# Six DMA issues on SyncE made to wait for an earlier transfer's landing, in a fused linear-attention and gated-FFN kernel

## The chip, the core and the metric

The kernel runs on one core of a Trainium2 chip. The metric is the device time of one execution in microseconds (us). The core has five engines that run side by side: TensorE (PE, matmuls, with its weight loads listed as PEld), VectorE (DVE), ScalarE (ACT), GpSimd (POOL) and SyncE (SP), which here issues all DMA transfers of data.

## The reference

A linear attention with a decaying state is followed by an FFN with a convolution gate:

```python
# r, k, v: (4, 8, 768, 48); w, u: (8, 48)
for t in range(S):
    cur = einsum('bhd,bhe->bhde', u * k[t], v[t])
    y[t] = einsum('bhd,bhde->bhe', r[t], state + cur)
    state = w * state + einsum('bhd,bhe->bhde', k[t], v[t])
x = y.transpose(0, 2, 1, 3).reshape(4, 768, 384)
h = maximum(x @ w_in, 0)                  # w_in: (384, 1024)
c = sum(conv_w[j] * shift(h, j - 1) for j in range(3))   # along the sequence
out = (h * sigmoid(c)) @ w_out            # w_out: (1024, 384)
```

All is float32; the weights reach the chip as 64-bit words.

## The kernel before

**Tiling.** The sequences are cut into 24 groups of 128 positions (four batches of six), each of two chunks of 64. For a group the kernel loads the decayed products' inputs: KR (keys and queries with the head dimension on the partitions, 448 KB), and KV (keys and values with positions on the partitions; a value half is 96 KB, a pair of key and query halves 192 KB). Three buffers of each rotate. `prep` scales KR on DVE and makes keys and diagonal terms, `scores`, `additions` and `outputs` give the 64-column matmuls on PE (L494), `chain` carries the state, and `split` copies the result as a high and a low part into XT (L548 on ACT, L549 on DVE).

**The FFN** runs over 7 units of up to 510 positions and 8 slices of the hidden dimension: `first` (L580) multiplies XT with w_in, ACT and DVE make relu, convolution and gate, and `second` (L609) multiplies with w_out, three slices later. The weights come in 8 pieces of w_in (two DMA halves of 192 KB) and 8 of w_out (384 KB) into the three buffers ST. `convert` turns each piece into float32 on ACT (L348, L354, L364), DVE (L356, L358) and DVE or POOL (L207). All pieces are loaded and converted in the first 70 us, between the attention of the first groups.

**What sets the order.** Every operation is recorded by `Plan.op` with a number. The table ORDER, written out by hand, lists these numbers; a letter behind a number picks the engine where several can do it. `Plan.order` reads the table, and a loop at the end of `rwkv_ffn_kernel` emits the operations one by one. Each engine runs its own in the order in which they come. Every data DMA goes through L211 on SP, in the table's order, so an issue that has to wait holds all later ones. An issue waits for the engines that still use its buffer. It also waits for the eighth last issue to have landed, since the issues take turns on eight semaphores (DMAHW0 to DMAHW7).

**Names.** In the rows below `KR<-in_krd_dram`, `KV<-in_vt_dram`, `KV<-in_krt_dram`, `ST<-in_w_in_dram`, `ST<-in_w_out_dram` and `uu<-in_ut_dram` are these loads. `HP<-DW,KR` (L393), `psY<-KR,SS` and `PO<-RS,KV` (L494) are attention matmuls of the first groups, `HP<-XT,wi` (L580) is the FFN's first product.

Of the kernel before, what the change touches and what calls it, by code (L numbers as in the profile page):

```python
# [61 lines left out]
144 277a 117 276 130p 119 128 293a 334 143 292 151d 297 191 335 129a 278 126 274d 279 294 125 213 149 192 341 193 148
295 194 296p 131 195 214 215 152 138p 134 216 132 196 280p 133a 197 135 217 169p 259 139 165 168 147 170p 218 140a 219
260 137 281 261 154p 141 299a 171 220 262 298 157p 155 263 337a 360 300 264 164 282 265 336 221d 198 366 338 283 199d
343a 325 166 158 161 284 159p 359 342 162 172p 163 266 160 305 156 403 326 176p 304 167 285 301 267p 303 327 339 348
328 286 340p 329 173a 174 287 344 302d 347 183 186d 330 350 361 249 189p 331 178 181 175 362a 182 187p 177 368a 349
421 179 288 394 180 185 367 351 404 289d 352 369 235 395 363 345 353 396 346p 364 397 370 373 251 254p 354 240 372 252
355 241 374 365p 332 188 409 244 405a 356 410 190p 237 246 238a 242 423a 357 422 243 247 333d 245 411 358p 412 413 429
427 428 406 371d 459 460 458 239 257p 398 399 236 400 414 407 415 416 417 401 449 255p 308p 256 258a 408p 418 461 424
419 425 402p 470 471 250 315 184 248 316 253 306 472 317 384 385 314 318 450 451 462 463 426p 420p 516 320p 452 453  # L70
454 464 465 466 455 456 467 468 517 501 502 513 519 510 321p 469p 309 310d 323d 307 311 503 312 377a 319 313 514 520
521 375 504 505 322 387 383 440 386 439 389p 457p 530 522 523 511 528 557 506 378 507 548 381 524 382 525 560 379d 388
324a 508 549 550 392p 380 376 430 438 441 551 552 553 390p 444p 391 554 590 509p 559 432d 393d 443 433 561 436 526 562
555 434a 431 437 435 563 591 592 593 564 565 483 445p 447p 571 529 558 473 479 475a 491 442 492 515 556p 496p 497d
499d 566 567 480 594 446 527p 595 476 477p 495 596 478 570 600 602 601 569 599 611 613 448a 481 474 482 531 543p 603
604 597 598p 568d 644 656 642 605 606 498 607 608 609 500p 533p 532 535 536 494 490 542 534 486 485 484 493 488 487
489 539 518 581 512 537 538 540 541 633 634 635 636 637 610p 546p 544p 667 545 645 646 572 624 582 579 612 583 638 639
685 654 700 643 655 694 697 647 648 649 650 574 651 703 547p 686 687 577 695 573 584 585p 586d 588p 640 652 641p 580
653p 628p 629p 575d 576 688 689 690 578 587 691 616a 614 734 701 698 713 714 712 617 704 705 706 707 692 693d 631d 708
709 746 744 627 756 735 736 620 618a 737 619 738 621 589p 630 615 747 748 743 699 676 623 622 675 626 625 702 739 710  # L80
729d 749 740 657 724 777 745 678 725 677 674 663 680p 681p 659p 750 664 670 671 668 751 752 682 732p 632p 683p 711p
757 789 787 741 778 665 666 660 779 780 781 661p 662 679 742p 799 658 755 786 782 790 791 717a 730p 792 793 783 794
715 721 718 753 795 722 728 719a 772p 773p 684p 673 672 669 818 830 775d 720 716 731 760p 754p 758 819 796 820 784 774
821 822 823 824 785p 831 832 761 833 834 797p 733d 759 762p 763 764 835 836 788 828 840 825 868 869 870 767 723 771
776a 800 829 841 798 883 886 887 826d 803d 726 768 765 770 769 809 766 727 801 858 827 839 808 813p 871 872 812 814d
816p 873 888 874 889 917 837 805 815 890 817p 838p 891 875 918 919 880 810 807 696 863p 866p 864p 806 802 804 842 847
849 907 859 908 955p 958p 912p 920 921 892 865 848 862 877 884 844 881 878 922 913p 956p 860 855 854 811 852 856 851
857 879 853 929 923 930 897 895 928 896 960 927 876d 940 931 932 933 924 934 935 972 926 938 893 894d 961 845a 962 850
# [12 lines left out]
1208 1226 1227 1228 1229 1197p 1238 1239 1240 1230 1231 1211 1222 1223 1232 1235 1236 1234 1185 1156 1155 1158 1188
1154 1241 1209p 1242 1243 1233d 1153 1182 1157 1249 1250 1251 1252 1253 1254 1261 1247 1259 1248 1255 1262 1244 1263
1264 1273 1271 1260 1246 1265 1266 1256 1257p 1267 1294 1274 1275 1276 1277 1245p 1278 1268 1295 1296 1279 1297 1298
1272 1286 1287 1289 1306 1299 1269p 1307 1308 1309 1310 1300 1311 1258 1280 1270 1282 1283 1290 1291 1318 1293 1292
1288 1281p 1312 1330 1304 1305 1316 1303 1315 1327 1319 1320 1321 1322 1331 1323 1301 1324 1313 1325 1332 1342 1343
1344 1333 1326d 1334 1345 1346 1328 1302p 1339 1314p 1317 1351 1354 1329 1340 1341 1352 1335 1336 1347 1337 1338p 1355
1358 1348 1349 1350d 1363 1353 1357 1364 1360 1284 1285 1361 1356 1359 1365 1366 1362 1367 1368
"""


class Plan:
# [29 lines left out]
    def order(self):  # L141
        seq, where, done = [], [None] * len(self.ops), set()
        for word in ORDER.split():
            if word == "f":
                seq.append(-1)
                continue
            i = int(word.rstrip("adp"))
            dur, x, pred, fn, cls = self.ops[i]
            assert done.issuperset(pred), (i, cls)
            where[i] = {"a": "act", "d": "dve", "p": "pool"}.get(word[-1]) or next(iter(dur))  # L150
            seq.append(i)
            done.add(i)
        assert len(done) == len(self.ops)
        self.seq, self.where = seq, where
        return seq, where


def rwkv_ffn_kernel(tc, krd, krt, vt, wd, ut, w_in, conv_w, w_out, out):
# [4 lines left out]
    with ExitStack() as ctx:  # L163
# [578 lines left out]
```

## Time and profile before

| | |
|---|---|
| median of 3 runs | 295.09 us (294.67 to 295.52) |
| the profiled execution | 298.1 us, its span 296.4 us |
| mean granted TensorE clock | 0.988 of full speed |
| busy: PE, PEld, DVE, ACT, POOL | 282.3, 244.5, 232.7, 192.1, 133.3 us |
| DMA | 37.47 MB, mean 126 GB/s |

The span runs from the first to the last instruction of the program; the execution's own time has some 1.7 us around it. The views used below are these. The page's first part gives each engine's busy time with the number of its instructions, and its third part the DMA queues. A timeline lists an engine's instructions by start, and in brackets how long the engine had been idle and what ended that; "issue" means that no wait in the profile explains the idle time. A view of stretches gives, for each stretch, every engine's busy time with the count of its instructions, then the granted TensorE clock, the DMA engines' busy share and GB/s. A DMA view of a short window lists what packets it holds by queue (q1 carries data, q8 instructions), and the issues in it with the time from issue to landing.

### The profile page before, as it was taken

The numbers are of one execution on the slowest core, as the hardware profiler recorded it, in microseconds if no ns is written. First come the engines' busy times: TensorE is split into PE (matmuls) and PEld (weight loads), VectorE is DVE, ScalarE is ACT, GpSimd is POOL, SyncE is SP. The second block draws the span as 40 slices with busy tenths as digits, with TensorE's granted clock in tenths as the row PEclk, the third lists the DMA queues.
The fourth block names the chain that finished last, engine by engine and source line by source line (L and its number), as shares of the span: only waits on it lengthen the run. The fifth ranks groups of instructions, "written<-read, shape, count | busy, mean of one in ns | idle before, by whom it ended". The sixth has DMA issues, their size and how long they took to land. (4 is left out here: it accounts for less than half of the span.)

```text
span 296.4 us, 10390 instructions
## 1 busy us (share of the span) xinstructions
PE 282.3 (95%) x4368; PEld 244.5 (82%) x4368; DVE 232.7 (79%) x399; ACT 192.1 (65%) x456; POOL 133.3 (45%) x157
## 2 busy tenths in 40 slices
PE   8778899979999999999999999999999999999995
PEld 6678898979998987878787878887888888888894
DVE  5878799997899988798989887896855875665550
ACT  3447499988797744774665666855456656575662
POOL 4111155668776474648762447173132460321321
PEclk9979799999999999999999999999999999999999
DMA  6958997986346667274453556413433000120021
GB/s 177 240 176 214 222 232 182 238 185 176 107 104 186 170 168 193 72 205 103 100 153 105 135 147 171 130 45 106 139 74 97 2 0 17 35 86 0 35 74 55
DMA packets 18642, 37.47 MB, mean 126 GB/s; under 512 B 3874, under 2 KB 10532, under 8 KB 18596
## 3 DMA queue, kind: packets, MB, share of 16 engines
q1 hardware_dynamic: 18596, 36.82, 47.7%
q8 instruction: 34, 0.56, 0.8%
q14 instruction: 12, 0.10, 0.1%
HBM read 30.01 MB, written 4.72 MB: 117 GB/s over the span
## 5 line engine op out<-in xcount | busy, mean ns | idle before, releaser
L580 PE MATMUL HP<-XT,wi 128*128 128x512 f32 (+3 forms) x504 | 111.4, 367 | 3.2 <-DVE SG L592 1.6
L580 PEld LDWEIGHTS HP<-XT,wi 128*128 128x128 f32 x504 | 88.0, 188 | 18.8 <-DVE SG L592 2.7
L609 PE MATMUL PO<-GH,wo 128*128 128x510 f32 (+3 forms) x336 | 102.0, 363 | 0.0
L588 DVE SCALAR_TENSOR_TENSOR CV<-HP,cw,CV 128x510 f32<-128x510 f32 (+3 forms) x112 | 74.9, 672 | 22.7 <-ACT CV L585 21.0
L207 POOL TENSOR_TENSOR GL<-SG,GH 128x510 fp32r<-128x510 f32 (+3 forms) x39 | 45.6, 1177 | 76.9 <-ACT GH L594 60.0
L609 PEld LDWEIGHTS PO<-GH,wo 128*128 128x128 f32 x336 | 61.3, 188 | 8.5
L609 PE MATMUL PO<-GL,wo 128*128 128x510 f32 (+3 forms) x168 | 60.6, 360 | 0.0
L591 ACT ACTIVATE SG<-CV 128x510 f32<-128x510 f32 (+3 forms) x56 | 32.0, 572 | 41.4 <-DVE CV L588 37.1
L592 DVE TENSOR_TENSOR SG<-HP,SG 128x510 f32<-128x510 f32 (+3 forms) x56 | 34.2, 611 | 13.2 <-ACT SG L591 12.7
L494 PE MATMUL psY<-RS,KV 64*48 64x64 f32 x720 | 43.7, 222 | 0.1
L494 PE MATMUL psY<-KR,SS 48*48 48x64 f32 x660 | 40.4, 217 | 0.4 <-issue 0.4
L584 ACT ACTIVATE HP<-HP 128x512 f32<-128x512 f32 (+3 forms) x56 | 29.3, 523 | 16.9 <-PE HP L580 16.3
L585 ACT ACTIVATE CV<-HP,cw 128x510 f32<-128x510 f32 (+3 forms) x56 | 35.1, 626 | 1.3
L594 ACT CAST GH<-SG 128x510 fp32r<-128x510 f32 (+3 forms) x56 | 30.6, 552 | 7.2 <-DVE SG L592 7.2
L609 PEld LDWEIGHTS PO<-GL,wo 128*128 128x128 f32 x168 | 31.6, 188 | 3.8 <-POOL GL L207 0.2
L207 DVE TENSOR_TENSOR KR<-KR,TKR 112x1024 f32<-112x1024 f32 x24 | 33.4, 1391 | 0.4 <-ACT TKR L322 0.4
L494 PEld LDWEIGHTS psY<-RS,KV 64*48 64x48 f32 x720 | 32.7, 122 | 0.5 <-issue 0.5
L494 PEld LDWEIGHTS psY<-KR,SS 48*48 48x48 f32 x660 | 31.0, 121 | 0.5 <-issue 0.5
L494 PEld LDWEIGHTS psA<-KR 48*64 48x64 f32 x704 | 22.3, 135 | 7.5 <-DVE RS L511 2.7
L433 POOL TENSOR_SCALAR_AFFINE_SELECT RS<-QQ 64x512 f32<-64x512 f32 x24 | 16.4, 685 | 23.4 <-DVE QQ L414 13.0
L494 PE MATMUL psA<-KR 48*64 48x64 f32 x704 | 25.5, 221 | 0.9 <-DVE RS L511 0.6
L548 ACT CAST XT<-psY 112x512 fp32r<-112x512 f32 (+9 forms) x27 | 13.8, 515 | 11.7 <-PE psY L494 11.5
(113 smaller groups left out, 358.7 us busy)
## 6 DMA issues: line engine op xcount, KB each, us to landing
KR<-in_krd_dram SPq DMA_DIRECT2D x24, 448.0 KB, 5.0
KV<-in_krt_dram SPq DMA_DIRECT2D x40, 192.0 KB, 4.0
KV<-in_vt_dram SPq DMA_DIRECT2D x48, 96.0 KB, 4.5
ST<-in_w_in_dram SPq DMA_DIRECT2D x16, 192.0 KB, 5.1
ST<-in_w_out_dram SPq DMA_DIRECT2D x8, 384.0 KB, 6.8
XT<-XT SPq DMA_DIRECT2D x24, 64.0 KB, 3.4
out_dram<-OS SPq DMA_DIRECT2D x6, 255.0 KB, 3.3
out_dram<-OS SPq DMA_DIRECT2D x3, 251.0 KB, 2.2
```

The source lines that it names most:

```text
L207: op(eng, d, rd, wr, lambda e: e.tensor_tensor(**kw), cls, port=True)
L433: G.affine_select(out=RS[j][o:o + 64], in_=QQ[j][o:o + 64].unsqueeze(2).broadcast_to([64, NP * 2, C]), pattern=[[0, NP * 2], [1, C]], comp ...
L494: PE.matmul(y, a, b_, start=s0, stop=s1)
L548: op("act", 0.06 + n / 1200.0, [key], cols("X", a + d, b + d), lambda e, xh=xh, v=v: A.copy(xh, v), "XH")
L580: PE.matmul(hp, wi[a][:, j, fs], XT[:, x, j, t], start=(j == 0 and k == 0), stop=(j == 2 and k == 2))
L584: op("act", 0.093 + n / 1200.0, [], [H_], lambda e: A.activation(hp, hp, AF.Relu, scale=1.0 / WS))
L585: op("act", 0.158 + n / 1200.0, [H_, "cw"], [("T", ti)], lambda e: A.activation(t1, hp[:, 1:n + 1], AF.Copy, scale=cw[:, 3 * f + 1:3 * f + ...
L588: op("dve", 0.117 + n * 1.085e-3, [H_, "cw"], [("T", ti)], lambda e, k=k: V.scalar_tensor_tensor(out=t1, in0=hp[:, k:n + k], scalar=cw[:, ...
L591: op("act", 0.11 + n / 1200.0, [("T", ti), "sgt"], [("SG", ti)], lambda e: A.activation(sg, t1, AF.Sigmoid))
L592: op("dve", dps(n), [H_], [("SG", ti)], lambda e: V.tensor_tensor(out=sg, in0=hp[:, 1:n + 1], in1=sg, op=ALU.mult), "GG")
L594: op("act", act(n), [("SG", ti)], [("GH", gi)], lambda e: A.copy(gh, sg))
L609: PE.matmul(PO[m][:, :n], wo[a][:, f, ms], g2[x], start=(f == 0 and k == 0), stop=(f == NF - 1 and k == 2))
```

## The change

A number in ORDER may now carry `w` and a count. Such an operation, a DMA on SP, gets a dependency on an earlier DMA of SP: with `w3` on the third last one before it. It is issued only when that one has landed. Six numbers get one: operations 2, 41, 275 and 121 `w3`, 223 `w5`, 99 `w2`. Sequence, engines and all other numbers of the table are as they were.

```diff
-17 0 26 12 8 15 10 9 1 16 21 4 14 11 20 5 27 23 18 2 22 13 43 19 35 33 3 31 37 44 32 50 34 80 55 79 38 28 39 40 63 29
-58d 41 36 6 71 56 30 74d 59 45 52d 46a 57a 47 201 200 48 75 82a 7 49d 60 51 81 62d 223 83 72 65 207 76 61a 78p 53 222
+17 0 26 12 8 15 10 9 1 16 21 4 14 11 20 5 27 23 18 2w3 22 13 43 19 35 33 3 31 37 44 32 50 34 80 55 79 38 28 39
+40 63 29 58d 41w3 36 6 71 56 30 74d 59 45 52d 46a 57a 47 201 200 48 75 82a 7 49d 60 51 81 62d 223w5 83 72 65 207
...
-        self.ops, self.port, self.last_w, self.last_r = [], [], {}, {}
+        self.ops, self.port, self.last_w, self.last_r, self.back = [], [], {}, {}, {}
...
+            word, _, back = word.partition("w")
             i = int(word.rstrip("adp"))
+            if back:
+                self.back[i] = int(back)
...
+        sent = []
         with tc.manual_schedule(engines={x.engine for x in eng.values()}):
...
-                    plan.ops[i][3](eng[where[i]])
+                    ins = plan.ops[i][3](eng[where[i]])
+                    if where[i] == "sp":
+                        sent.append(ins.ins)
+                        if i in plan.back:
+                            tc.add_manual_dep(ins.ins, sent[-1 - plan.back[i]].name, mybir.DependencyInfo(
+                                mybir.DependencyClass.Sync, mybir.DependencyReason.DATA), reason="pace")
```

On PE, DVE, ACT and POOL the same instructions stand in the same order with the same waits. On SP the order is the same too, and only the waits differ. Of SP, from the second KR load on (KR1 for the second group, KV0 to KV2 the buffers of the first three), before:

```order
L211 DMA KR1_62<-in_krd_dram 112x1024
L211 DMA KV0_64<-in_vt_dram 64x384
L211 DMA ST0_95<-in_w_in_dram 64x768
...
L211 DMA ST2_97<-in_w_in_dram 64x768 [waits DMAHW1_49]
L211 DMA ST2_97<-in_w_in_dram 64x768 [waits DMAHW2_49]
L211 DMA KR2_63<-in_krd_dram 112x1024 [waits DMAHW3_49]
L211 DMA KV2_66<-in_vt_dram 64x384 [waits DMAHW4_49]
L211 DMA KV1_65<-in_vt_dram 64x384 [waits DMAHW5_49]
```

and now:

```order
L217 DMA KR1_62<-in_krd_dram 112x1024
L217 DMA KV0_64<-in_vt_dram 64x384 [waits DMAHW1_49]
L217 DMA ST0_95<-in_w_in_dram 64x768
...
L217 DMA ST2_97<-in_w_in_dram 64x768
L217 DMA ST2_97<-in_w_in_dram 64x768 [waits DMAHW2_49]
L217 DMA KR2_63<-in_krd_dram 112x1024 [waits DMAHW3_49]
L217 DMA KV2_66<-in_vt_dram 64x384 [waits DMAHW4_49,DMAHW1_49]
L217 DMA KV1_65<-in_vt_dram 64x384 [waits DMAHW5_49]
```

The KV0 load waits for the first KR load (DMAHW1), which the first w_in half of ST2 then needn't name again; the KV2 load waits for that w_in half, the next user of DMAHW1.

Of SP some 20 issues later, at the w_out load of ST2 and the uu behind it, before:

```order
L211 DMA KV1_65<-in_krt_dram 64x768 [waits DMAHW1_49,PE_49]
L211 DMA KV1_65<-in_krt_dram 64x768 [waits PE_49]
L211 DMA ST2_97<-in_w_out_dram 128x768 [waits DMAHW3_49,Activation_49]
L211 DMA uu_123<-in_ut_dram 64x192 [waits DMAHW4_49]
...
L211 DMA KR1_62<-in_krd_dram 112x1024 [waits DMAHW0_49,PE_49]
L211 DMA KV0_64<-in_vt_dram 64x384 [waits DMAHW1_49]
```

and now:

```order
L217 DMA KV1_65<-in_krt_dram 64x768 [waits DMAHW1_49,PE_49]
L217 DMA KV1_65<-in_krt_dram 64x768 [waits PE_49]
L217 DMA ST2_97<-in_w_out_dram 128x768 [waits DMAHW3_49,DMAHW0_49,Activation_49]
L217 DMA uu_123<-in_ut_dram 64x192 [waits DMAHW4_49,DMAHW1_49]
...
L217 DMA KR1_62<-in_krd_dram 112x1024 [waits PE_49]
L217 DMA KV0_64<-in_vt_dram 64x384 [waits DMAHW7_49]
```

The w_out load waits for the w_in half three issues before it (DMAHW0), the uu load for the first of the two KV loads, and the KV0 load for the issue two before it (DMAHW7).

## Rows read from the trace of the kernel before

**Rows 1.** The page, parts 1 (busy us) and 3 (packets, MB, share).

```profile
PE 282.3 (95%) x4368; PEld 244.5 (82%) x4368; DVE 232.7 (79%) x399; ACT 192.1 (65%) x456; POOL 133.3 (45%) x157
...
q8 instruction: 34, 0.56, 0.8%
```

**Rows 2.** Timeline of PE: start us, us, instruction, idle before it.

```profile
15.95 0.37 PE L393 MATMUL HP<-DW,KR 48*64 48x48 f32 x5 [2.98 <-issue]
...
21.47 0.26 PE L494 MATMUL psY<-KR,SS 48*48 48x64 f32 x2 [0.39 <-issue]
...
30.43 0.21 PE L494 MATMUL PO<-RS,KV 64*48 64x64 f32 x1 [1.83 <-issue]
...
66.61 0.62 PE L580 MATMUL HP<-XT,wi 128*128 128x384 f32 x2 [1.49 <-POOL wi L207]
```

**Rows 3.** Stretches from the start: PE busy (x), PEld busy (x), then DVE, ACT, POOL.

```profile
0.00:8.49 8.49, 7.20 (x95) 5.60 (x97) 4.73 (x14) 3.00 (x7) 3.39 (x17) 1.00 0.73 186
...
0.00:12.95 12.95, 11.51 (x222) 9.56 (x222) 8.53 (x22) 5.63 (x15) 3.39 (x17) 1.00 0.82 201
...
0.00:29.00 29.00, 23.79 (x603) 21.44 (x604) 21.32 (x46) 14.26 (x42) 7.54 (x25) 0.94 0.77 200
0.00:186.43 186.43, 175.83 (x3266) 154.58 (x3269) 162.15 (x281) 128.28 (x326) 100.54 (x125) 0.98 0.65 165
```

**Rows 4.** DMA queues, window 13.2 to 13.4; none of q8 from 8.4 to 13.2.

```profile
q8 instruction: 1, 0.02, 39.4%
```

**Rows 5.** DMA queues, window 27.5 to 27.7; none of q8 from 25.0 to 27.5.

```profile
q8 instruction: 1, 0.02, 36.8%
```

**Rows 6.** DMA queues, window 187.1 to 187.3; none of q8 from 171.6 to 187.1.

```profile
DMA packets 1, 0.02 MB, mean 82 GB/s; under 512 B 0, under 2 KB 0, under 8 KB 0
...
q8 instruction: 1, 0.02, 38.8%
```

**Rows 7.** Stretches after the three stops: after five engines, granted clock, DMA share, GB/s.

```profile
16.00:22.00 6.00, 5.61 (x151) 5.46 (x154) 5.03 (x9) 3.07 (x9) 0.91 (x2) 0.72 0.57 178
30.00:36.00 6.00, 5.57 (x145) 5.57 (x146) 3.95 (x8) 1.88 (x7) 1.27 (x1) 0.72 0.93 217
65.00:70.00 5.00, 3.51 (x20) 3.39 (x20) 3.17 (x7) 3.36 (x8) 4.78 (x6) 1.00 0.42 96
```

**Rows 8.** Timeline of SP: issues by start, with the issue's own time.

```profile
1.28 0.40 SPq L211 DMA_DIRECT2D KR<-in_krd_dram  x1
...
2.81 0.53 SPq L211 DMA_DIRECT2D KV<-in_vt_dram  x1
...
5.93 1.10 SPq L211 DMA_DIRECT2D ST<-in_w_in_dram  x2
7.49 0.32 SPq L211 DMA_DIRECT2D KR<-in_krd_dram  x1
7.88 1.28 SPq L211 DMA_DIRECT2D KV<-in_vt_dram  x2
```

**Rows 9.** Tile KR, 0 to 10 us: the three loads, from issue to landing.

```profile
DMA to landing us min/median/max: 3.4/5.0/5.9
```

**Rows 10.** DMA issue of 5.93: KB, us to landing.

```profile
ST<-in_w_in_dram SPq DMA_DIRECT2D x1, 192.0 KB, 4.9
```

**Rows 11.** DMA issue of 19.33, on an empty queue: KB, us to landing.

```profile
ST<-in_w_out_dram SPq DMA_DIRECT2D x1, 384.0 KB, 3.1
```

**Rows 12.** Stretches, columns as in rows 3 and 7.

```profile
15.17:36.10 20.93, 17.93 (x530) 17.55 (x530) 15.44 (x30) 10.92 (x34) 3.73 (x7) 0.84 0.77 201
...
18.00:24.00 6.00, 5.61 (x166) 5.46 (x166) 4.70 (x12) 2.68 (x10) 0.85 (x2) 0.78 0.42 107
24.00:46.00 22.00, 19.47 (x440) 18.32 (x435) 19.13 (x36) 17.37 (x52) 8.40 (x11) 0.92 0.98 237
...
36.00:66.00 30.00, 28.25 (x577) 25.97 (x572) 29.33 (x56) 29.05 (x79) 16.78 (x18) 1.00 0.93 215
```

**Rows 13.** Timeline of DVE, the XT subtraction of the third group.

```profile
36.10 0.56 DVE L549 TENSOR_TENSOR XT<-psY,XT 128x384 fp32r<-128x384 f32 x1 [2.12 <-ACT XT L548]
```

More of the change, by code (lines that the diff above doesn't have):

```diff
@@ L62 @@
[L62 to L76, printed above, removed]
@@ new lines @@
+112 111 121w3 230 212p 231d 113a 24 25 227 97 291 270 114 290 232 115a 271d 122 233 136 272 116a 120 234d 99w2
+228d 118 145 150d 273 153d 146 127 100 142 144 277a 117 276 130p 119 128 293a 334 143 292 151d 297 191 335 129a
+278 126 274d 279 294 125 213 149 192 341 193 148 295 194 296p 131 195 214 215 152 138p 134 216 132 196 280p 133a
+197 135 217 169p 259 139 165 168 147 170p 218 140a 219 260 137 281 261 154p 141 299a 171 220 262 298 157p 155
+263 337a 360 300 264 164 282 265 336 221d 198 366 338 283 199d 343a 325 166 158 161 284 159p 359 342 162 172p
@@ new lines @@
+163 266 160 305 156 403 326 176p 304 167 285 301 267p 303 327 339 348 328 286 340p 329 173a 174 287 344 302d 347
+183 186d 330 350 361 249 189p 331 178 181 175 362a 182 187p 177 368a 349 421 179 288 394 180 185 367 351 404
+289d 352 369 235 395 363 345 353 396 346p 364 397 370 373 251 254p 354 240 372 252 355 241 374 365p 332 188 409
+244 405a 356 410 190p 237 246 238a 242 423a 357 422 243 247 333d 245 411 358p 412 413 429 427 428 406 371d 459
+460 458 239 257p 398 399 236 400 414 407 415 416 417 401 449 255p 308p 256 258a 408p 418 461 424 419 425 402p
@@ new lines @@
+712 617 704 705 706 707 692 693d 631d 708 709 746 744 627 756 735 736 620 618a 737 619 738 621 589p 630 615 747
+748 743 699 676 623 622 675 626 625 702 739 710 729d 749 740 657 724 777 745 678 725 677 674 663 680p 681p 659p
+750 664 670 671 668 751 752 682 732p 632p 683p 711p 757 789 787 741 778 665 666 660 779 780 781 661p 662 679
+742p 799 658 755 786 782 790 791 717a 730p 792 793 783 794 715 721 718 753 795 722 728 719a 772p 773p 684p 673
+672 669 818 830 775d 720 716 731 760p 754p 758 819 796 820 784 774 821 822 823 824 785p 831 832 761 833 834 797p
@@ new lines @@
+915d 1037 925p 1152 965 966 969 939 898 882 906 950 1003 936 973 974 867a 975 861 951 976 977 911 937d 967 968p
+900a 901 978 904 1004 1005 899 957 914 902d 981 970 1015 1016 979 1012 971 983 905 1006 1007 903 1008 941 993
+949 952 980p 998p 954 1009 943d 1050 910 909 1010 944 1017 1018 959p 916p 947 1019 1011d 1020 1021 1051 1052
+1053 1054 942 945p 982 1014 1026 1071 1024 1059 1055 1060 1013 1025 1063 1072 1073 946 997 948 984 986p 1074
+1075 1056 987 988d 1022 1023p 1064 990 985 1076 1077 991 989 1061 1067 1080 1083 1078 1084 1085 1081 1001d 953
@@ new lines @@
+1027 1033 994 1045d 885 1068 1086 1087 1034 1088 1035 1057 1089 1058p 1101 1082 1092 1094 1113 1093 1102 1103
+1104 1105 1106 1079p 1107 1108 1114 1115 1116 992 1125 1112 1111 1124 1110 1122 1090 1091p 1029a 1117 1036 1118
+1119 1126 1127 1040 1070 1038 1042 1066 1041 996 1039 1069 1062 1043 1044 999d 1030 1031p 1032 1137 1138 1136
+1123 1128 1129 1120 1130 1131 1135 1134 1097p 1109p 1046p 1147 1148 1139 1132 1140 1141 1000 1133d 1142 1143
+1144 1145p 1048p 1159 1160 1161 1171 1172 1121d 1146 1168 1180 1169 1002d 1028 1162 1163 1164 1173 1165 1189
@@ new lines @@
+1174 1175 1047 995 1095 1183 1166 1176 1167p 1049p 1177 1201 1096 1099 1100 1065 1190 1191 1181 1192 1098 1193
+1194 1170 1186 1149 1187 1195 1213 1198 1184 1210 1199 1202 1203 1204 1205 1206 1196 1214 1150 1207 1151 1225
+1200 1212 1215 1216 1217 1178 1179p 1224 1218 1219 1237 1220 1221d 1208 1226 1227 1228 1229 1197p 1238 1239 1240
+1230 1231 1211 1222 1223 1232 1235 1236 1234 1185 1156 1155 1158 1188 1154 1241 1209p 1242 1243 1233d 1153 1182
+1157 1249 1250 1251 1252 1253 1254 1261 1247 1259 1248 1255 1262 1244 1263 1264 1273 1271 1260 1246 1265 1266
@@ new lines @@
+1256 1257p 1267 1294 1274 1275 1276 1277 1245p 1278 1268 1295 1296 1279 1297 1298 1272 1286 1287 1289 1306 1299
+1269p 1307 1308 1309 1310 1300 1311 1258 1280 1270 1282 1283 1290 1291 1318 1293 1292 1288 1281p 1312 1330 1304
+1305 1316 1303 1315 1327 1319 1320 1321 1322 1331 1323 1301 1324 1313 1325 1332 1342 1343 1344 1333 1326d 1334
+1345 1346 1328 1302p 1339 1314p 1317 1351 1354 1329 1340 1341 1352 1335 1336 1347 1337 1338p 1355 1358 1348 1349
+1350d 1363 1353 1357 1364 1360 1284 1285 1361 1356 1359 1365 1366 1362 1367 1368
```

51 lines of the change are left out of this document (17 added, 34 removed).

## The prediction

> **What bounds the kernel now.** I read the page first: TensorE (PE) is busy for 95% of a span of 296.4 us, so what is lost on it is lost at the end [rows 1]. The same page lists a DMA queue of its own for instructions, q8: 34 packets, 0.56 MB. PE executes 4368 matmuls and 4368 weight loads, 8736 in all: 257 for each packet. So q8 brings PE its own program, in blocks of about 256.
>
> Then I looked for the places at which PE stands still. Its timeline shows three stops that end in "issue", that is, with no wait that the profile knows: 2.98 us before 15.95, 0.39 before 21.47, 1.83 before 30.43 [rows 2]. Counting PE's instructions explains them: 444 had run at the first stop (222 and 222) and 1207 at the third, 763 more, which is three blocks of 256 less the semaphore waits that the view leaves out [rows 3]. PE stops at block ends, because the next block has not come.
>
> When is a block asked for? Where no data is on the way, the packet follows the start of the block before it at once: 6535 instructions (444 and 24 blocks, less their waits) had run at 186.43, and the window from 187.1 holds a packet and nothing else [rows 3, 6], some 0.7 us later. At the first stop 192 had run by 8.49, one block less than at 12.95 [rows 3]; yet the packet starts only in the window from 13.2 [rows 4], 4.7 us later. What lay ahead is on SP's timeline: 448 KB of KR issued at 7.49 and two KV transfers from 7.88 [rows 8]. The third stop has the same pattern: its packet starts in the window from 27.5 [rows 5]. So program blocks queue behind data that was issued too early.
>
> The stops cost twice. In 16 to 22 us and in 30 to 36 us the granted clock was 0.72 of full speed, between its two levels of 1.2 and 2.4 GHz: 6 us times 0.28 is 1.7 us each time. After the idle of 1.49 us that ended at 66.61 it stayed at 1.00 [rows 2, 7]. In all 2.98 + 0.39 + 1.83 + 1.7 + 1.7 = 8.6 us of PE.
>
> **The change part by part.** No instruction moves and none is added on an engine; six DMA issues on SP get one wait more, and some older waits fall away as implied. SP issues in order, so all that stands behind a held transfer is held too.
>
> *First wait* (the first KV half waits for the first KR). That KR is issued at 1.28 and lands 3.4 us later, at 4.7 [rows 8, 9], so the KV goes out at 4.7 and not at 2.81. Behind it on SP stand four issues of about 0.6 us and the pair at 5.93; the train ends near 8.9 and not at 7.03, 1.9 us later. The KR of 7.49 leaves at about 8.9. Cover: the second KR, issued before it, has 448 KB and keeps the queue busy for 1.9 us after the first one's landing, at 237 GB/s [rows 12], to 6.6; a transfer moves about 1.5 us after its issue (3.1 us to land on an empty queue, less 1.6 us for its 384 KB [rows 11, 12]), the held KV at 6.2. So the data lands as before.
>
> *Second wait* (KV of 7.88 waits for the first w_in half of 5.93). That one lands 4.9 us after its issue, at 10.8 [rows 10]; both KV transfers leave from 10.8 and not from 7.88. In front of them KR2 is then still moving, so again nothing runs dry. Behind them stand the two w_in halves of the next piece, up to 1.9 us later than before. ScalarE, which reads them, was busy for 10.92 of the 20.93 us from 15.17 to 36.10 [rows 12] and can make this up; I take nothing, with 1.9 us as the bound.
>
> What both do together: at 8.49, when PE asks for its block, neither KR2 nor the two KV transfers are on the queue. They are 448 + 192 = 640 KB, at 237 GB/s [rows 12] 2.7 us. The packet should start near 10.6 instead of 13.3. *Term 1:* the stop of 2.98 shrinks by 2.7 to 0.3 us. *Term 2:* an idle of 1.49 us left the clock at 1.00 and one of 2.98 did not, so with 0.3 the slow stretch of 16 to 22 us goes as well: 1.7 us. Together 4.4 us.
>
> *Third wait* (a w_in half, op 223, waits for that KV). The KV itself and four more issues of 0.6 us stand before it, so SP gets there near 13.8. The KV lands at 13.9 if it takes the 3.1 us of an empty queue [rows 11], at 15.7 if it takes 4.9 us as in [rows 10]: a hold of 0.1 to 1.9 us, for a weight piece with the same half idle reader. I take zero.
>
> *Fourth and fifth* (a w_out, op 275, and the uu behind it, op 121), *sixth* (a KV half, op 99). The fourth leaves 384 KB in flight, 1.6 us of work; the sixth 448 KB, 1.9 us. A transfer on an empty queue lands after 3.1 us, 1.5 of which nothing moves, so the worst holes, if nothing else is queued, are 3.1 - 1.6 and 3.1 - 1.9, 2.7 us in all; the best is zero. DMA was busy for 0.98 of 24 to 46 [rows 12], so a backlog covers most of it: I take 0.5. The fifth hides behind the fourth, whose 384 KB are then in flight too. Whether these waits help the third stop the trace can't say, since what lies ahead of that packet moves with everything else. Bounds: 0 and 1.83 + 1.7 = 3.5 us; I take 0, the nearest row being the stop as it is [rows 2, 5].
>
> **What limits the gain.** VectorE (DVE) was busy 15.44 of the 20.93 us from 15.17 to 36.10, so it can follow by 5.5 us at most. DMA was busy 0.42 of 18 to 24, idle for 3.5 us, and then nearly full to 46. From 36 to 66 ScalarE (29.05 of 30) and DVE (29.33) are full too [rows 12]: they run the weights' conversion, fed by DMA. They keep a head start, but only as far as DMA delivers: 3.5 us is all that can be pulled into the idle. So the sum is 4.4, capped at 3.5, less 0.5 for holes: **3.0 us**. From 66 on PE sets the pace and passes this on to the end.
>
> The profiled execution took 298.1 us, 1.7 more than its span, and the runs shown have a median of 295.09. 298.1 - 3.0 = 295.1 for the profiled one; from the median, **292.1**. Should the 3.0 us between the two lie in the stops, 5.6 of the 8.6 us are there without a profile, and the gain is 2.0: 293.1.
>
> **A rule against it.** The packet of 13.3 came after the data issued before it [rows 4, 8]. The Trainium skill, DMA: Bandwidth & Descriptors, section "Queues, rings and completion order", says that each DMA engine takes turns between its queues packet by packet; by that a block would not wait behind another queue's data. The Trainium skill, Runtime: NRT & Kernel Launch, section "Instruction fetch mechanics", gives blocks of 16 KiB, which the trace bears out (0.56 MB in 34), and calls their cost mostly hidden, which the 2.98 us contradict. By these rules the sum would be 0.
>
> **The rivals.**
> - *The packets take turns and do not queue behind data.* The stop then has another cause, and earlier or later issues change nothing: gain 0, cost 0 to 0.5, 295.1 to 295.6. Against it: 0.7 us on a quiet queue and 4.7 on a full one. Chance 0.05.
> - *The gain is given back.* PE waits again before 66.61 for a weight piece from GpSimd [rows 2]; if that is tied to DMA, full by then, the head start only lengthens this wait. Time 294.4 to 295.9. Chance 0.18.
> - *Slower: holes in a full queue.* If pulled-forward use thins the backlog, the fourth and sixth wait each leave DMA dry for 1.2 to 1.5 us in a stretch whose transfers feed full engines: 2.7 us lost. It decides once the gain left by the other stops is below 1.8 us, for instance when the block after the first meets the held KV transfers and PE stops there instead. Then 295.1 - 0.5 + 2.7 = 297.3. Chance 0.13.
> - *More:* the third stop goes too, and the gain reaches DVE's 5.5 us: 289.6. Chance 0.12.
>
> **How the numbers follow.** Forecast 292.1, its own band 290.3 to 294.2, chance 0.52. About 0.3% (0.9 us) is what a measurement of this kernel can tell from no change. Faster: 0.52 + 0.12 = 0.64; within: 0.05 + 0.18 = 0.23; slower 0.13. The range takes in the larger gain and the case given back: 289.5 to 295.9.
>
> **What would show it.** In the changed kernel's trace the first q8 packet should start near 10.6, the stop of 2.98 be under 0.6 and the clock in 16 to 22 us be 1.00; the XT subtraction on DVE at 36.10 [rows 13] should come at 32 to 33. If the packet stays near 13, term 1 is wrong; if it moves and the clock still falls, term 2. If DMA is clearly below 0.98 between 24 and 46 the holes are real; if the PE wait before 66.61 grows by the gain, the second rival holds.

## The result, and the profile after

The changed kernel takes **298.65 us** (median of 9 runs, 296.76 to 300.26); the kernel before took 295.26 beside it (9 runs, 293.90 to 296.39). The ratio is **1.011, 95% interval 1.0074 to 1.0147**: 3.2 us slower, where 3.0 us faster was predicted. The sign was wrong, and the time lies above the range (289.5 to 295.9). Here and below a ratio compares only executions within 1.5% of the fastest of their kernel, which leaves out more of before's than of the others', so it can lie up to 0.3% above the quotient of the medians (e14: 1.0089, medians 296.90 and 295.14).

The profiled execution of the changed kernel took 298.26 us (span 296.6), that of before 298.1 (span 296.4). The two pages can therefore hardly differ, and yet the kernels do: the profile of before shows an execution 3 us above its median, the profile after one at its own. A trace of the changed code without any of the six waits (e1, below: 294.2 us, span 292.5) is the better partner, and stands beside it here. One thing in it is not alike: its first 37 matmuls took 3.11 us and those of after 4.09 (last section), so about 1 us of what separates the two traces does not come from the waits. A second trace of the changed kernel (e9: 2.88 us there, span 295.8) is given where that matters.

The page of after, parts 1 and 3, which answers to [rows 1]:

```profile
PE 283.0 (95%) x4368; PEld 244.6 (82%) x4368; DVE 234.0 (79%) x399; ACT 192.4 (65%) x456; POOL 132.9 (45%) x157
...
q8 instruction: 34, 0.56, 0.8%
```

The DMA queues of after in the window 9.4 to 9.6; no q8 packet lies between 0 and 9.3. It answers to [rows 4], where the packet came at 13.2 to 13.4:

```profile
q8 instruction: 1, 0.02, 35.6%
```

The timeline of PE in after: every idle time of 0.3 us and more between 8 and 47 us (start, duration, instruction, idle before it), which answers to [rows 2]:

```profile
15.65 0.33 PE L500 MATMUL psY<-RS,VP 64*64 64x64 f32 x4 [0.60 <-DVE RS L517]
18.94 0.87 PE L500 MATMUL HP<-KV 64*48 64x48 f32 x29 [1.01 <-DMA KV<-in_vt_dram]
23.05 1.97 PE L500 MATMUL PO<-KR 48*64 48x64 f32 x32 [0.66 <-ACT QQ L415]
33.47 1.13 PE L399 MATMUL psU<-DW,KR 48*64 48x48 f32 x32 [1.11 <-DVE SS L536]
45.12 1.84 PE L586 MATMUL HP<-XT,wi 128*128 128x384 f32 x9 [2.03 <-DVE SG L598]
```

No line says "issue" any more: the program arrives in time, as meant. In place of the three stops of before (2.98 + 0.39 + 1.83 = 5.20 us) stand five waits for data and for the engines that work on it: 0.60 + 1.01 + 0.66 + 1.11 + 2.03 = 5.41 us. (Before has one such wait too, 0.65 us at 45.11, shown further down.) The last one has a cause that can be read off. PE waits for SG; DVE makes SG (L598) right after its product KR (L213), and that one waited for a load. DVE in after, then SP in after (when it issued what):

```profile
43.04 1.56 DVE L213 TENSOR_TENSOR KR<-KR,TKR 112x1024 f32<-112x1024 f32 x1 [1.06 <-DMA KR<-in_krd_dram]
```

```profile
24.20 1.18 SPq L217 DMA_DIRECT2D KV<-in_krt_dram  x2
28.77 0.33 SPq L217 DMA_DIRECT2D ST<-in_w_out_dram  x1
...
32.73 0.58 SPq L217 DMA_DIRECT2D KR<-in_krd_dram  x1
35.05 0.47 SPq L217 DMA_DIRECT2D KV<-in_vt_dram  x1
...
38.05 0.53 SPq L217 DMA_DIRECT2D KR<-in_krd_dram  x1
```

Two holes stand in SP's line: 25.38 to 28.77, the fourth wait (op 275, w_out), and 33.31 to 35.05, the sixth (op 99, KV). The KR load of the sixth group is issued at 38.05. In e1, without these holes, it goes out at 32.00, and DVE does not wait. SP, then DVE, of e1:

```profile
32.00 0.33 SPq L217 DMA_DIRECT2D KR<-in_krd_dram  x1
```

```profile
40.43 1.39 DVE L213 TENSOR_TENSOR KR<-KR,TKR 112x1024 f32<-112x1024 f32 x1
```

e9, the changed kernel again, with the shorter first matmuls, has the same chain. DVE, then PE, of e9:

```profile
42.67 1.57 DVE L213 TENSOR_TENSOR KR<-KR,TKR 112x1024 f32<-112x1024 f32 x1 [0.94 <-DMA KR<-in_krd_dram]
```

```profile
44.76 1.84 PE L586 MATMUL HP<-XT,wi 128*128 128x384 f32 x9 [1.72 <-DVE SG L598]
```

Stretches of after (after the five engines: granted clock, DMA share, GB/s), then of e1:

```profile
12.00:16.00 4.00, 3.40 (x122) 3.29 (x120) 2.94 (x6) 2.13 (x9) 1.68 (x2) 1.00 0.49 144
...
20.00:28.00 8.00, 7.34 (x169) 7.18 (x167) 7.40 (x16) 5.39 (x17) 2.07 (x5) 0.57 0.88 223
28.00:30.00 2.00, 2.00 (x76) 2.00 (x74) 0.97 (x3) 1.21 (x4) 0.00 (x0) 1.00 0.31 70
...
36.00:38.00 2.00, 2.00 (x16) 1.75 (x15) 1.75 (x4) 1.97 (x5) 0.00 (x0) 1.00 0.59 157
24.00:46.00 22.00, 18.57 (x404) 17.55 (x401) 18.67 (x35) 16.86 (x51) 9.61 (x13) 0.92 0.81 207
```

```profile
12.00:16.00 4.00, 3.35 (x114) 3.12 (x112) 3.41 (x7) 2.59 (x10) 2.12 (x3) 1.00 1.02 237
...
28.00:30.00 2.00, 1.72 (x60) 1.57 (x56) 1.97 (x5) 1.67 (x6) 0.00 (x0) 1.00 0.92 239
30.00:36.00 6.00, 4.68 (x44) 4.59 (x45) 5.00 (x9) 3.18 (x8) 1.27 (x1) 0.72 1.03 238
36.00:38.00 2.00, 2.00 (x34) 1.75 (x34) 1.36 (x3) 1.86 (x5) 0.66 (x1) 1.00 1.01 203
```

The holes are there as DMA share: 0.49, 0.31 and 0.59 in after, where e1 has 1.02, 0.92 and 1.01. From 24 to 46 it is 0.81, against 0.98 in [rows 12] and 0.95 in e1; but e15, a second trace without any wait, has 0.83 there, so this mean alone shows no holes, and SP's timeline has to. And the clock still falls, to 0.57 from 20 to 28, which costs 8 × 0.43 = 3.4 us, as much as the two slow stretches of [rows 7] (1.7 each).

All of the difference from e1 is made in the first 79 us. PE of e1, then of after, the same feed-forward matmuls:

```profile
42.34 1.85 PE L586 MATMUL HP<-XT,wi 128*128 128x384 f32 x9 [0.53 <-DVE SG L598]
...
74.75 1.86 PE L586 MATMUL HP<-XT,wi 128*128 128x388 f32 x9 [0.34 <-DVE SG L598]
```

```profile
78.80 1.51 PE L586 MATMUL HP<-XT,wi 128*128 128x388 f32 x7 [0.55 <-DVE SG L598]
```

After is 2.8 us behind e1 at 45.12 (about 1 us of it from the first matmuls), 4.05 at 78.80, and 4.1 at the end (296.6 less 292.5). e9 is 2.4 us behind at its 44.76.

Beside the traced execution of before, the same matmul shows where the head start goes. DVE of after at the subtraction of [rows 13], then PE of before:

```profile
33.79 0.55 DVE L555 TENSOR_TENSOR XT<-psY,XT 128x384 fp32r<-128x384 f32 x1
```

```profile
45.11 1.84 PE L580 MATMUL HP<-XT,wi 128*128 128x384 f32 x9 [0.65 <-DVE SG L592]
```

At the subtraction after is 2.31 us ahead (33.79 against 36.10); at the feed-forward matmul, 45.12 against 45.11, all of that is gone.

### The profile page after: what moved, and what is told of

The parts are those of the page before. It is cut to its first block, busy times and chain, and to the rows that moved or that the text cites. A ratio compares the mean times of both kernels' runs of the same rounds, so it can differ in the third digit from the quotient of the medians.

```text
span 296.6 us, 10390 instructions
## 1 busy us (share of the span) xinstructions
PE 283.0 (95%) x4368; PEld 244.6 (82%) x4368; DVE 234.0 (79%) x399; ACT 192.4 (65%) x456; POOL 132.9 (45%) x157
## 5 line engine op out<-in xcount | busy, mean ns | idle before, releaser
L213 POOL TENSOR_TENSOR GL<-SG,GH 128x510 fp32r<-128x510 f32 (+3 forms) x39 | 45.8, 1181 | 77.4 <-ACT GH L600 60.6
L598 DVE TENSOR_TENSOR SG<-HP,SG 128x510 f32<-128x510 f32 (+3 forms) x56 | 34.2, 611 | 13.1 <-ACT SG L597 12.6
L500 PE MATMUL psY<-RS,KV 64*48 64x64 f32 x720 | 42.5, 218 | 0.1
L500 PE MATMUL psY<-KR,SS 48*48 48x64 f32 x660 | 39.6, 215 | 0.0
L213 DVE TENSOR_TENSOR KR<-KR,TKR 112x1024 f32<-112x1024 f32 x24 | 33.5, 1396 | 1.7 <-DMA KR<-in_krd_dram 1.3
L500 PEld LDWEIGHTS psY<-RS,KV 64*48 64x48 f32 x720 | 31.7, 119 | 0.6 <-issue 0.6
L500 PEld LDWEIGHTS psY<-KR,SS 48*48 48x48 f32 x660 | 30.2, 119 | 0.0
L439 POOL TENSOR_SCALAR_AFFINE_SELECT RS<-QQ 64x512 f32<-64x512 f32 x24 | 17.9, 744 | 24.2 <-DVE QQ L420 13.0
L213 POOL TENSOR_TENSOR KV<-KV 128x384 f32<-128x384 f32 x16 | 17.6, 1099 | 7.6 <-DMA KV<-in_krt_dram 4.6
```

The source lines that it names most:

```text
L213: op(eng, d, rd, wr, lambda e: e.tensor_tensor(**kw), cls, port=True)
L439: G.affine_select(out=RS[j][o:o + 64], in_=QQ[j][o:o + 64].unsqueeze(2).broadcast_to([64, NP * 2, C]), pattern=[[0, NP * 2], [1, C]], comp ...
L500: PE.matmul(y, a, b_, start=s0, stop=s1)
L598: op("dve", dps(n), [H_], [("SG", ti)], lambda e: V.tensor_tensor(out=sg, in0=hp[:, 1:n + 1], in1=sg, op=ALU.mult), "GG")
```

## The experiments

All kernels are the changed kernel's code with other waits or another order in its table; everything is computed. "w3" behind an op means that it is issued when the third last transfer before it has landed. Of the table only the words around an edit are shown. Each ratio is to runs of the kernel before on the same chip, with its 95% interval. e16 and e18 have 4 executions, e9 and e10 have 6, the others 10 to 12. The 18 runs:

| run | waits and order | median us | ratio |
|---|---|---|---|
| e1, e15 | none | 294.20, 294.96 | 0.9985 (0.9951 to 1.0018), 1.0029 (0.9988 to 1.0069) |
| e2 | first | 296.19 | 1.0040 (1.0006 to 1.0074) |
| e3 | second | 295.86 | 1.0029 (0.9992 to 1.0067) |
| e4, e18 | fourth to sixth | 297.83, 297.89 | 1.0104 (1.0066 to 1.0142), 1.0110 (1.0034 to 1.0187) |
| e5 | sixth | 296.87 | 1.0055 (1.0026 to 1.0085) |
| e6 | fourth and fifth | 295.82 | 1.0030 (0.9992 to 1.0068) |
| e7, e17 | one, at KR | 296.90, 296.83 | 1.0052 (1.0020 to 1.0084), 1.0081 (1.0042 to 1.0119) |
| e8 | one, behind KR | 295.37 | 0.9999 (0.9965 to 1.0034) |
| e9 | all six | 299.33 | 1.0124 (1.0080 to 1.0168) |
| e10 | all six, KR ahead of the sixth | 300.15 | 1.0157 (1.0121 to 1.0194) |
| e11 | one, at the third KR load | 296.44 | 1.0034 (1.0007 to 1.0061) |
| e12 | first, conv load ahead of it | 296.14 | 1.0030 (1.0003 to 1.0058) |
| e13 | three, behind KR | 295.43 | 1.0033 (0.9990 to 1.0075) |
| e14, e16 | none, KR issued late | 296.90, 297.71 | 1.0089 (1.0051 to 1.0127), 1.0111 (1.0031 to 1.0190) |

### Which wait costs: e1 to e6

e1 takes all six waits out:

```diff
-18 2w3 22
+18 2 22
-58d 41w3 36
+58d 41 36
-62d 223w5 83
+62d 223 83
-226 275w3 92a
+226 275 92a
-111 121w3 230
+111 121 230
-234d 99w2
+234d 99
```

> The changed code with none of the six waits: the kernel before again, in the changed kernel's wrapping. Both theories: same time as before, within 0.3%. What it is for: a second trace of that sequence. If the stops of 2.98 and 1.83 us and the two stretches at a clock of 0.72 are what a usual execution has, they stand here again within 0.3 us; if the first profile showed them longer than usual (it was 3 us above the median), they are shorter here, together under 5.6 us in place of 8.6.

Measured: 294.20, the same as before, so the waits alone make the loss. PE's stops in e1:

```profile
12.59 0.49 PE L399 MATMUL HP<-DW,KR 48*64 48x48 f32 x9 [0.32 <-issue]
...
17.49 0.26 PE L500 MATMUL psY<-KR,SS 48*48 48x64 f32 x2 [0.63 <-issue]
26.17 0.21 PE L500 MATMUL PO<-RS,KV 64*48 64x64 f32 x1 [1.28 <-issue]
31.32 1.65 PE L399 MATMUL psU<-DW,KR 48*64 48x48 f32 x32 [1.60 <-DVE SS L536]
```

Without any wait the stop that carried term 1 is 0.32 us here, not 2.98 (in e15, the same code again, it is 2.17). The three stops and the one stretch at a clock of 0.72 come to 0.32 + 0.63 + 1.28 + 1.7 = 3.9 us, under the 5.6 expected. And where the stops are short, PE next waits 1.60 us for DVE.

e2, e3 and e4 are e1 with one part put back:

```diff
-18 2 22
+18 2w3 22
```

> Only the first wait (operation 2). Theory A (the holds let DMA run dry, each for as long as its hold, and the program blocks gain less than that): one early hold of 1.9 us, covered by the second KR, so the first program block comes early (near 10 us in place of 13) and little is lost: 1 to 2.5 us faster, 292.8 to 294.3. Theory B (taking PE's stop away is worth nothing, because the data of the next step come no earlier): the packet comes early all the same, the time stays within 0.9 us of before.

```diff
-58d 41 36
+58d 41w3 36
```

> Only the second wait (operation 41). Theory A: SP is held from 7.9 to 10.8 us; the KR ahead of it covers only 2 us of that, so the KV and w_in behind it land 1 to 2 us later; the first program block still waits behind that KR and comes near 12; 0.5 to 2 us slower, 296 to 297. Theory B: within 0.9 us.

```diff
-226 275 92a
+226 275w3 92a
-111 121 230
+111 121w3 230
-234d 99
+234d 99w2
```

> Only the fourth, fifth and sixth waits (operations 275, 121, 99). Theory A: the first stop of 2.98 us stays as it is; the three holds stop SP for 2 to 3 us each between 26 and 36 us, DMA's share of 24 to 46 falls from 0.98 to about 0.85, and the engines that convert weights get them late: 2 to 4 us slower, 297 to 299. Theory B: the loss of the whole change comes from the early waits; these three cost under 0.9 us.

No part gains. The first wait does what it was meant to do, with no "issue" stop of 0.3 us or more before 46 us, and its median is 1.1 us above that of before. Its ratio of 1.0040 is little more than the 1.0029 of e15, which has no wait at all, so its own loss is hardly shown beyond the noise; that of the second, 0.29% with an interval that reaches zero, is not. In e2, DVE, ScalarE and then PE:

```profile
11.64 0.18 DVE L362 TENSOR_SCALAR TT<-ST 128x24 int32<-128x24 int32 x1 [1.60 <-DMA ST<-in_conv_w_dram]
```

```profile
11.54 0.56 ACT L354 ACTIVATE CC<-ST 128x384 f32<-128x384 f32 x1 [5.03 <-DMA ST<-in_w_in_dram]
```

```profile
16.29 0.33 PE L500 MATMUL psY<-RS,VP 64*64 64x64 f32 x4 [1.47 <-DVE RS L517]
```

The conv load stands four issues behind the held KV, and DVE waits for it (0.34 us in e1). But this wait is not the one that is passed on: DVE's next instruction comes at 12.57, after 0.76 us more for ScalarE, and ScalarE had waited until 11.54 for a w_in half, which stands behind the held KV as well. In e1 ScalarE starts there at 10.41, 1.13 us sooner, and PE's matmul of 16.29 comes at 15.13. At the feed-forward matmul of 42.51 e2 is only 0.17 us behind e1 (42.34), so its trace does not show where the rest of its time goes. The last three waits carry most: 2.8 us over the median of before. In e4, SP, DVE and PE:

```profile
38.32 0.53 SPq L217 DMA_DIRECT2D KR<-in_krd_dram  x1
```

```profile
43.08 1.61 DVE L213 TENSOR_TENSOR KR<-KR,TKR 112x1024 f32<-112x1024 f32 x1 [0.95 <-DMA KR<-in_krd_dram]
```

```profile
45.21 1.85 PE L586 MATMUL HP<-XT,wi 128*128 128x384 f32 x9 [1.78 <-DVE SG L598]
```

It is the chain of after again. e5 and e6 divide the three:

```diff
-234d 99
+234d 99w2
```

> Only the sixth wait (operation 99). Theory A (one hold decides: it stops SP for 4 us near 31 to 35 us, the KR load of the sixth group four issues behind it leaves 3 to 6 us later, DVE waits for that KR and PE for DVE): 2 to 3.3 us slower, 297 to 298.4, with DVE waiting some 1 us for KR near 42 us. Theory B (each hold costs the DMA time that it leaves empty, wherever it stands): about a third to a half of the last three together, 1 to 1.5 us slower, 296 to 296.6.

```diff
-226 275 92a
+226 275w3 92a
-111 121 230
+111 121w3 230
```

> Only the fourth and fifth waits (operations 275 and 121). Theory A: their holds of 2 to 4 us delay weights and the uu vector, which have room; under 1 us slower, 295 to 296. Theory B: 1.5 to 2 us slower, 296.5 to 297.

The sixth costs 0.55%, the fourth and fifth 0.30% (the interval reaches zero); together 0.85%, and 1.04% was measured for the three. The KR wait that Theory A expected in e5 is not in its trace: SP stands still for 0.9 us only, and DVE's KR product comes at 42.20 without a wait.

### What a wait costs: e7 to e10

e7 and e8 are e1 with one new wait each, at the KR load of the sixth group (op 144), or at the issue right behind it (op 334, a w_in piece):

```diff
-142 144 277a
+142 144w2 277a
```

> None of the six waits; instead the KR load of the sixth group itself (operation 144, the fourth issue behind operation 99) waits for the second last issue before it, which holds SP from about 32 to 37.6 us with this KR and all behind it. Theory A: the loss of the last three waits comes back without them, 2 to 4 us slower, DVE waiting for KR near 42 us. Theory B: DMA is left empty for some 3 us less its cover, 1 to 1.5 us slower.

```diff
-293a 334 143
+293a 334w3 143
```

> The same hold one issue later: the w_in half behind that KR (operation 334) waits for the third last issue, the same transfer as in the run before; SP is held from about 33 to 37.6 us, but the KR has left. Theory A: at least 1.5 us faster than the run before, within 1 us of the kernel before. Theory B: the same time as the run before within 0.9 us, since the same bytes are held back nearly as long.

The hold that catches KR costs 0.52%, the hold one issue later nothing (0.9999). So it isn't the hold alone; what stands behind it matters. The trace of e7 does not show this, though. The KR load, held to 35.78 and with little ahead of it on the queue, landed in 3.9 us, at 39.7; in e1 the one of 32.00 took 7.9 us, to 39.9. DMA issues of e7, then of e1, with us to landing:

```profile
KR<-in_krd_dram SPq DMA_DIRECT2D x1, 448.0 KB, 3.9
```

```profile
KR<-in_krd_dram SPq DMA_DIRECT2D x1, 448.0 KB, 7.9
```

The result of e7 and e8 still suggested sending KR ahead of the sixth wait (e10), with the changed kernel again beside it (e9, no edit):

> The changed kernel once more, beside the three others of this batch, so that they are compared on one chip. Both theories: 298.3 to 299.0 us, 1.0 to 1.2% over before.

```diff
-234d 99w2
+234d 144 99w3
-142 144 277a
+142 277a
```

> The changed kernel with all six waits; only the KR load of the sixth group (op 144, which stood behind the transfer with the sixth wait, op 99) is issued ahead of it, so that op 99 still waits for the landing of the same uu load, with the KR load now its second predecessor. Theory A (the last waits cost because a later KR load sits behind them in SP's order, and DVE and then PE wait for it at 42 to 45 us): KR lands about 3 us earlier, those two waits go, and the kernel is 1.5 us or more faster than e9 (about 297). Theory B (the cost is in the thinner flow of data as a whole, whichever load is last): within 0.9 us of e9.

My theory fell here: e10 is no faster than e9, 300.15 against 299.33. PE of e10, and a stretch:

```profile
41.84 1.51 PE L500 MATMUL psU<-KV 64*48 64x48 f32 x30 [1.83 <-DMA KV<-in_vt_dram]
```

```profile
42.00:46.00 4.00, 4.00 (x38) 3.91 (x37) 2.55 (x4) 1.01 (x4) 3.59 (x4) 0.50 1.08 222
```

KR is there, and now PE itself waits 1.83 us for a V load that KR overtook, and the clock goes to 0.50 behind it. A reading that fits: the loads from op 120 to op 144 (KR of the fifth and sixth group and the KV loads between them) are all needed by about 42 us; with the holes ahead of them the set is late as a whole, and order only chooses which member.

### Two attempts at a better version: e11 and e12

e11 holds nothing but the third KR load (op 40), to let the first program block pass; e12 is e2 with the conv load (op 50) ahead of the held KV:

```diff
-39 40 63
+39 40w3 63
```

> None of the six waits; only the third KR load (op 40) is issued when the conv load, three issues ahead, has landed, so that the first block of program requested in the span finds the queues with less ahead of it and nothing but this one load of the first group is held. Theory A (the gain of the first wait, no 0.4 to 3.0 us stop, is real, and what it loses is conv and w_in landing late): 0 to 1.5 us faster than before, with the stop under 0.5 us and no wait of DVE for the conv load. Theory B (the stop is a delay that data pays in another place anyway): within 0.9 us of before.

```diff
-18 2w3 22
+18 50 2w4 22
-32 50 34
+32 34
```

> The first wait alone, as in e2_first_wait, but the conv load (op 50) is issued ahead of the held transfer instead of behind it; the hold is still for the landing of the first KR load. Theory A (e2 lost because the conv load sat behind the hold, and DVE waited 1.6 us for it): that wait goes and the kernel is about 1 to 1.5 us faster than e2, about 295. Theory B (the KV and w_in loads behind the hold are late as well, and set the pace by themselves): the same as e2, about 296.2.

Neither gains: 296.44 and 296.14, the latter the time of e2. In e12 DVE no longer waits for conv, but ScalarE waits for the w_in load behind the hold as it did in e2 (11.54 there):

```profile
11.98 0.55 ACT L354 ACTIVATE CC<-ST 128x384 f32<-128x384 f32 x1 [4.68 <-DMA ST<-in_w_in_dram]
```

PE's stop of 1.47 us behind it stays as in e2, at 16.71. So the w_in load was the one that mattered, not conv, as Theory B had it. No version here beats the kernel before.

### Is it the set that is late, or the holes? e13 to e18

e13 has three waits of the depths of e4, on the three issues behind KR; e14 has no wait, but KR moved behind those three issues:

```diff
-293a 334 143 292 151d 297 191 335 129a
+293a 334w3 143 292 151d 297w3 191 335w2 129a
```

> Three waits of the depths of e4_last_three (third, third, second last landing), but on the three issues directly behind the KR load of the sixth group (w_in, w_out, w_in, ops 334, 297 and 335) instead of ahead of it; no other wait. Theory A (what costs in the last three waits is that the set of K, R and V loads due by 42 us lands late as a whole, whatever its order): these three cost nothing, within 0.9 us of before. Theory B (three waits cost wherever they stand, since a thinner flow of data costs clock or loads later on): the loss of e4, 2 to 4 us over before.

```diff
-142 144 277a
+142 277a
-191 335 129a
+191 335 144 129a
```

> No wait at all; only the KR load of the sixth group (op 144) is issued behind the three loads that followed it (ops 334, 297 and 335), so that it lands some 3 us later (near 43 instead of 39.9) while the DMA engines stay full. Theory A (the lateness of that set is the price): DVE waits for KR near 41 us as in after and the kernel is 1 us or more over before. Theory B (idle DMA engines, not the place of KR, are the price): within 0.9 us of before.

Three holds behind the set cost nothing that can be told from zero (1.0033, 0.9990 to 1.0075), while one late member costs 0.89% with the DMA engines full. SP and DVE of e13:

```profile
33.38 0.53 SPq L217 DMA_DIRECT2D KR<-in_krd_dram  x1
37.42 0.47 SPq L217 DMA_DIRECT2D ST<-in_w_in_dram  x1
```

```profile
40.64 1.39 DVE L213 TENSOR_TENSOR KR<-KR,TKR 112x1024 f32<-112x1024 f32 x1
```

SP stands still for 3.5 us, the DMA share is only 0.41 to 0.64 in each 2 us from 36 to 44, and DVE is on time. But the trace of e14 did not show DVE waiting for KR, as I had expected; DVE, itself late behind a PE at a slow clock, got to its KR product only at 42.49, just as KR landed (issued at 34.48, 8.0 us to landing). So four kernels were traced a second time:

> The changed code without any wait, as e1_no_waits, for a second trace on the chip of the next three. Both theories: within 0.9 us of before; one slow stretch of the granted clock near 32 to 35 us, as in e1, and DVE's KR product near 40.4 without a wait.

> As e14_kr_late, for a second trace: the first had the loss of time (2.6 us) but not the wait for KR; its granted clock stood at 0.50 from 32 to 38 us. Theory A (KR's lateness is the price): DVE's KR product waits for its load or comes at 42 or later, with the clock as in e15. Theory B (what the order of the loads costs is a longer slow stretch of the clock before KR is used): again 0.50 from 32 to 38, and KR no later than its reader. Both: 1 to 3 us over e15.

> As e7_hold_at_kr, for a second trace: the first had the clock at 0.50 from 32 to 38 us and no wait for KR, too. Theory A: KR product waiting or late, clock as in e15. Theory B: clock at 0.50 from 32 to 38 again. Both: 1 to 2.5 us over e15.

> The last three waits alone, as e4_last_three, for a second trace. Theory A (KR's lateness is the price): DVE waits about 1 us for KR at 42 to 43 us and PE about 1.8 us before 45, as in e4, 2.5 to 4 us over e15. Theory B: no such waits, the clock lower for longer instead.

e16 shows the wait. DVE and PE of e16:

```profile
43.21 1.23 DVE L213 TENSOR_TENSOR KR<-KR,TKR 112x1024 f32<-112x1024 f32 x1 [2.54 <-DMA KR<-in_krd_dram]
```

```profile
44.95 2.34 PE L586 MATMUL HP<-XT,wi 128*128 128x384 f32 x9 [2.99 <-DVE SG L598]
```

e17 and e18 show it as a remnant of 0.23 and 0.22 us, and e15, which has no wait in its code, suggests why. PE and DVE of e15:

```profile
15.29 0.49 PE L399 MATMUL HP<-DW,KR 48*64 48x48 f32 x9 [2.17 <-issue]
20.78 0.26 PE L500 MATMUL psY<-KR,SS 48*48 48x64 f32 x2 [1.90 <-issue]
```

```profile
43.16 1.50 DVE L213 TENSOR_TENSOR KR<-KR,TKR 112x1024 f32<-112x1024 f32 x1
```

The profiled execution of e15 took 298.46 us, the longest of its ten; their median is 294.96. It has long program stops, as that of before has, and DVE gets to its KR product only at 43.16. Where the stops are long (e15, e17, e18), data that lands at 43 is nearly in time; where they are short (e1: KR product at 40.43), it is 2 to 3 us late. Other traces fit. There are 14 in which nothing is held up to the third KR load. In six of them the first stop is 1.01 us or less: the three with KR issued by 33.5 us (e1, e6, e13) reach the feed-forward matmul that stood at 45.12 in after at 41.99 to 42.55, the three with KR late or held (e7, e14, e16) at 44.59 to 44.95. In the other eight the first stop is 1.89 us or more: before, e8 and e15 reach that matmul at 45.09 to 45.19, and e4, e17 and e18, with KR held, at 44.96 to 45.43, hardly later; e3 (42.62) and e5 (44.22) are faster. The holds thus take away the good executions: the shortest of before took 292.82 us, of e14 and e16 295.98, of e4 and e18 296.21, of after and e9 296.76. That is not all, since the longest of after and e9 is longer too, 300.72 against 298.86 of before.

What stays open: in e7 and e14, the clock stood at 0.50 from 32 to 38 us and the KR wait was absent. In e14 PE's stop ahead of that stretch, 2.46 us before 31.83 (1.60 in e1), can't come from the edit, which moves no issue before 32 us, and in e7 KR was not late. How much of their loss is the clock and how much the late load can't be told from one trace each. The wait for KR alone is in sight in e16, and together with the holes in after, e4 and e9.

## Why the prediction was wrong, point by point

- **What bounds the kernel** (program blocks queue behind data): right. With nothing of the computation changed, only data issued later, the packet moved from 13.2 to 9.4 (the prediction had 10.6), and no "issue" stop of 0.3 us or more is left before 47 us. The Trainium skill, DMA: Bandwidth & Descriptors, section "Queues, rings and completion order", has each engine take turns between queues by the packet; the two packet times do not agree with it, they follow the data ahead. That holds as far as PE asks for a block when the one before it starts, which the prediction read from the counts of instructions.
- **Term 1, 2.7 us**: mechanism right, size and effect wrong. The 2.98 us came from one execution 3 us above the median, and is the largest of 14 traces in which the early loads go out as before; e1 has 0.32. The prediction saw the possibility ("2.0") and took the larger figure all the same. And what is gained is not kept: in e1 PE stops at 31.32 for DVE.
- **First wait, "the data lands as before"**: this step failed in three of five traces. It counted bytes in flight, and asked whether the queue runs dry; it did not ask when each load behind the held one is due. In e2 a w_in half comes 1.13 us later for ScalarE than in e1, and PE is 1.16 us later at 16.29; in e10 and e12 the half is later still (12.01 and 11.98), but in after and e9 it is on time (10.14 and 10.18, 10.07 in before). Nor did the queue stay full: in after the DMA share is 0.72 from 6 to 8 us and 0.74 from 8 to 10, in e1 1.04 and 1.07. What the wait costs by itself is hardly above the noise (1.0040 for e2, 1.0029 for e15 without a wait).
- **Second wait, "again nothing runs dry"**: failed. SP was held to 12.10 in after, not to 10.8, and in e3, with this wait alone, the DMA share from 12 to 16 us is 0.61 (1.02 in e1, 1.00 in e2). Its cost is not shown to differ from nothing (e3, 1.0029, 0.9992 to 1.0067).
- **Term 2, 1.7 us**: failed. "1.49 us of idle left the clock at 1.00" was one row at 66 us, read as a rule. In after 0.60 and 1.01 us of idle were followed by a clock of 0.57 from 20 to 28 us: the slow stretch came later (0.90 in 16 to 22), it did not go.
- **Third wait, 0**: never tried by itself. In after SP was free for it at 15.99 and issued it at 16.09, so it held 0.1 us at most.
- **Fourth to sixth wait, 0.5 us (bound 2.7)**: the term that decided, mis-sized more than five times: 2.8 us by the medians of e4, 3.0 by those of e18. A DMA share of 0.98 was read as a backlog that covers holes. It is the other way round: a stretch with no spare DMA time, in which the loads behind a hole come later (KR issued at 38.05, 32.00 in e1). The step that failed is that the holes were priced as empty DMA time, while the runs show a price in the loads behind them: e8 and e13 have such holes where no load behind them is due soon, and cost nothing that can be told from zero; e14 and e16 have none, only the late KR, and cost 0.89 and 1.11%.
- **The rivals**: the one that came true is "holes in a full queue", at 0.13, with 297.3, outside the stated range. It named the place and the mechanism, and its condition, a gain below 1.8 us, was met by a gain near zero. It had the price of the holes as dry DMA time, where the measured price is a late set of loads. "The gain is given back" was looked for at the 66 us wait, too late: that wait of 1.49 us is in neither e1 nor after, and in e1 the gain is given back at 31.
- **The cap and the passing on**: right in form. After 79 us nothing changes: 4.05 us there, 4.1 at the end. A loss is passed on just as a gain would have been.

## What to carry to other kernels

Before pacing an issuing queue, list what stands behind the held transfer, and for each load when its reader needs it; here a hold was free only behind the last load that was due soon. A full DMA stretch is not cover for a hole: what stands behind the hole comes later. And look at the spread of the runs before pricing a stop from one trace: where the profiled execution lies 3 us above the median, its stops need not be the typical ones. Here the first one was 0.32 us in one trace and 2.17 in another of the same code.

## What the runs showed of the hardware that was not expected

The same code starts differently from one execution to the next. The 37 warm-up matmuls took 4.09 us in before and in e15, and 3.11 in e1. PE of before, then of e1:

```profile
2.54 4.09 PE L273 MATMUL PO<-wz 128*128 128x512 bf16 x37
```

```profile
2.54 3.11 PE L279 MATMUL PO<-wz 128*128 128x512 bf16 x37
```

With 4.09 the first stop was 2.98 (before) and 2.17 us (e15), with 3.11 it was 0.32. The 14 traces in which nothing is held up to the third KR load all divide in this way. In six the warm-up took 3.04 to 3.63 us, the first program packet came at 9.8 to 10.4, and the first stop was 0.32 to 1.01 us; in eight it took 3.92 to 4.09, the packet came at 12.0 to 13.4, and the stop was 1.89 to 2.98. A reading that fits is that PE then asks for its block before or after the large KR load is on the queue: 190 of its instructions had run by 7.70 in e1, with that load issued at 8.13, and 192 by 8.49 in before, with the load issued at 7.49. In after the warm-up took 4.09 as well, and there was no stop, since the loads were held. Why the warm-up differs, no run here shows.
